# Batch 1's queries and keys on SyncE's DMA queue, channel weights gated behind them, batch 2's loads on SyncE, stores on GpSimd's queue

## The chip, the cores and the metric

One core of a Trainium2 chip runs the whole program. The metric is the device time of one execution in microseconds (us), as the median of several runs; the kernel before takes 317.31 us (median of 3 runs, 316.95 to 317.64). One more execution was taken under the hardware profiler, and all rows of a profile here come from such an execution.

## The reference

For 8 batches of 576 positions, a local attention with 8 heads of 64 channels: position i attends to j where |i - j| <= 32, or where i or j is one of 8 global positions. Its output `x` (576 x 512 per batch) goes through an MLP mixer.

```
scores = scale * q @ k.T ; attn = softmax(where(mask, scores, -1e9)) ; x = attn @ v
h   = relu(x.T @ w_tok1) @ w_tok2 ;  u = x + h.T          # mixes positions
out = u + relu(u @ w_ch1) @ w_ch2                         # mixes channels
```

q, k, v and the output are 32-bit floats, 1.18 MB per batch and tensor; the work runs in 16-bit floats.

## The kernel before, in words

**One batch at a time, overlapped.** For each batch b the loop at L956 records operations: load q, k and v into 32-bit staging tiles (`lq`, `lk`: the first 512 positions, in two DMAs of four heads, 512 KB each; `lr`: the last 64 positions of q and k, two DMAs of 128 KB; `lv`: v in five tiles), cast them to 16 bit on ScalarE (ACT) or VectorE (DVE) (`qk`, `rn`, `vsh`; L534, L531, L546), transpose q and k, compute the scores (`scores`, L673 on TensorE, PE), their exponentials (`e`, L683 on ACT), the mask (L689 on DVE), the sums over global keys (`glob_sums`: L720, which reads all five tiles of `vsh` and every head's `eg`), `rf` (L726), the attention output (`values`: L740 and L753, then `x`, L781), then `token1` (L803), `token2` (L821, `u` at L834), the transposed u (`uT`, `uTl`), `chan1` (L866, relu at L858 on ACT or L860 on DVE, which makes `b1`), `chan2` (L895, the final sum `osb` at L903) and the store (L906, L909).

**Staging tiles exist once.** `lq`, `lk`, `lr`, `lv` and `qk` have one buffer each, so that a load of batch b+1 waits until batch b was cast. `qT`, `kT`, `vsh`, `e` and `x` have two, `osb` three. The channel weights `wc1` (three DMAs of 512 output columns) and `wc2` (three) are cast from 32 to 16 bit in the DMA, which is issued from GpSimd (POOL); the token weights `w1`, `w1l`, `w2` likewise.

**Transposes.** For batches 0 to 2 PE transposes q and k (L566, L585) and u (L848). For batches 3 to 7 the DMA does: SyncE (SP) issues `raw<-qk` (L643, eight per batch), `rawr<-rn` (L639), and DVE copies them into `qT` and `kT` (L651, L654, L646, L648); `uT<-u` (L853) from batch 3 on.

**Who sets the order.** Nothing is in source order. Each `op` has a priority, candidate engines with estimated costs, and the data it reads and writes. The planner `run` (L119 to L272) simulates the engines and DMA queues with its own figures and emits the instructions in the order of that simulation; on the chip each engine then runs its list strictly in order, and waits on semaphores for the data. An `op` can also name others that it goes `behind`: that shifts it in the planner's simulation, but no semaphore comes of it, so on the chip it holds only where both stand on one engine. A `gate` (L918) is a POOL copy of one element of a loaded tile into `hold`: it makes POOL wait until that load has landed, and holds back what POOL issues next.

**Queues before.** SP issues batch 0's q, k, v, the loads of batches 3 to 7 but v, all transposes by DMA and all stores. POOL issues the gate on batch 0's v, the token weights, the gathers of global rows (L487), batch 1's q and k, then `wc1`, one part of `wc2`, batch 1's v, the rest of `wc2`, and batch 2's q, k, v. ACT issues v of batches 3 to 7. In a profile the queue of SP is q1, of POOL q0, of ACT q10. DMAs of SP and ACT use eight semaphores in turn, those of POOL eight others, and an issue waits until the last DMA on its semaphore has landed.

Of the kernel before, what the change touches and what calls it, by code (L numbers as in the profile page):

```python
# [15 lines left out]
P = 128  # L16
# [11 lines left out]
def kernel(  # L28
# [12 lines left out]
    nc = tc.nc  # L41
    B, H, S, D = q.shape
# [844 lines left out]
    def chan2(b, tau, pri):  # L887
# [17 lines left out]
        if not last:  # L905
            op([("S", 0.45)], pri + 5, lambda e: nc.sync.dma_start(out=out[b, P * tau : P * tau + P, :], in_=osb), r=[("osb", o)], dma=STORE)  # L906
        else:
            for z in range(2):
                op([("S", 0.45)], pri + 5, lambda e, z=z: nc.sync.dma_start(  # L909
                    out=out[b - 1 + z, S - LAST : S, :], in_=osb[64 * z : 64 * z + 64]), r=[("osb", o)], dma=(0.39, 2048, 0.8, 64))  # L910
# [3 lines left out]
    PEB = 3  # L914
# [7 lines left out]
    def loads(b, n0=0):  # L922
        pl = 100.0 * b - 145 if b != 1 else -174.0
        if b == 0:
            load_rest(0, -196, [("S", 0.65)])
            for hs in (slice(0, 2), slice(2, 4), slice(4, 8)):
                for ti in range(2):
                    load_qk(0, ti, hs, -195 + hs.start, [("S", 0.6)])
            load_v(0, -180, [("S", 0.6)])
            gate(-178, [("lv", NT - 4)], [lv[:, NT - 4, 0, 0:1]])  # L930
            return
        if b < PEB:
            if b == 1:
                pl = -173.9
            load_rest(b, pl, [("G", 0.73)], [n0] if b == 1 else ())
            for h in range(0, H, 4):
                for ti in range(2):
                    load_qk(b, ti, slice(h, h + 4), pl + 1 + h / 2 if b > 1 else pl + 0.1 + h / 100, [("G", 0.88)], [n0] if b == 1 else ())
            if b > 1:
                load_v(b, pl + 6, [("G", 0.87)])  # L940
        else:
            load_rest(b, pl, [("S", 0.65)])
            for h in range(0, H, 4):
                for ti in range(2):
                    load_qk(b, ti, slice(h, h + 4), pl + 1 + h / 2, [("S", 0.5)])
            load_v(b, pl + 6, [("A", 0.6)])
# [9 lines left out]
    for b in range(B):  # L956
        base = 100.0 * b
        ca = base - 85
        if b != 1:
            loads(b)  # L960
        if b == 0:
# [3 lines left out]
            n2 = len(ops) - 1  # L965
            op([("G", 0.77)], -173, f_wc1(0), w=[("wc1", 0)], dma=(2.6, 4096, 2.0, 512), behind=[n0])
            op([("G", 1.0)], -174.5, f_w2, w=["w2"], dma=(2.4, 4096, 2.0, 512), behind=[n0])
            for t in (1, 2):
                op([("G", 0.77)], -173 + t, f_wc1(t), w=[("wc1", t)], dma=(2.6, 4096, 2.0, 512), behind=[n0])
            n1 = len(ops) - 1  # L970
        if b == 1:
# [3 lines left out]
        if b < 2:  # L975
            for ti in range(2):
                op([("G", 2.7)], (-115 if ti == 0 else -174.2) if b == 0 else 70, f_gather(b, ti), r=["idx"], w=[("g32", b, ti)], dma=(0.1, 256, 1.7, 256),
                   behind=[] if b == 0 and ti == 0 else [n2])
# [80 lines left out]
```

## Time and profile before

| | |
|---|---|
| median of 3 runs | 317.31 us |
| profiled execution: its own time, its span | 317.08 us, 315.4 us |
| PE busy | 291.4 us (92%) |
| DVE, ACT, POOL busy | 187.6, 178.7, 44.5 us |
| chain of work that ended last | PE 49%, DMA 24%, DVE 11%, ACT 10% |
| DMA traffic | 51.31 MB in 96452 packets |

Times inside the execution count from the start of the span. In a timeline row stand the start, the duration, the engine, the line of the kernel, the operation, what it writes and reads, the count of merged instructions, and in brackets the idle time ahead of it with what ended it. A row of a windows table gives each engine's busy time in that stretch, then TensorE's granted clock (1.00 is full speed), the mean busy share of the 16 DMA engines (which can exceed 1 where packets overlap) and GB/s.

### The profile page before, as it was taken

Reading aid. Unit: us, or ns where it says so; the run is one execution under the profiler, and the core shown is the slowest. Engines: PE = TensorE matmul, PEld = TensorE weight load, DVE = VectorE, ACT = ScalarE, POOL = GpSimd, SP = SyncE. Lnnn points to the kernel's source line nnn. Section 1 sums busy time; section 2 is a strip of 40 time slices with the busy share of each in tenths; the row PEclk is TensorE's granted clock in tenths of the full one; section 3 lists DMA queues with packets and bytes.
Section 4 is the critical chain, followed back from the end, with each engine's and each line's share of the span. In section 5 each row is a group of like instructions: output and inputs, shape, how many; then the busy total and the mean of one; then the engine's idle time right before and its main releaser. Section 6 shows DMA issues by size and latency. Waiting matters only on the chain.

```text
span 315.4 us, 7280 instructions
## 1 busy us (share of the span) xinstructions
PE 291.4 (92%) x2944; PEld 153.3 (49%) x2944; DVE 187.6 (59%) x413; ACT 178.7 (57%) x322; POOL 44.5 (14%) x81
## 2 busy tenths in 40 slices
PE   6968989997999898999999996799999999999993
PEld 3635645453474444444475443444465445444641
DVE  7588867569777587586675657772554257230021
ACT  4872895479996484965985693541832182305500
POOL 8588735620000000000000000000000000000000
PEclk9779999999999999799999999999999999999999
DMA  6999999999599979999999989415001401051013
GB/s 179 253 135 295 207 221 246 275 254 265 122 238 214 209 207 301 162 217 223 310 164 153 304 192 203 109 22 164 33 2 31 137 35 36 11 160 49 2 67 100
DMA packets 96452, 51.31 MB, mean 163 GB/s; under 512 B 73698, under 2 KB 89954, under 8 KB 96418
## 3 DMA queue, kind: packets, MB, share of 16 engines
q1 hardware_dynamic: 66512, 33.83, 48.7%
q0 software_dynamic: 6464, 11.11, 16.5%
q10 hardware_dynamic: 23442, 5.90, 9.9%
q8 instruction: 23, 0.38, 0.5%
q14 instruction: 11, 0.09, 0.1%
HBM read 36.11 MB, written 9.44 MB: 144 GB/s over the span
## 4 chain that ended last, share of the span: by engine, by line
PE 49%; DMA 24%; DVE 11%; ACT 10%; issue 2%; SPq 2%; ACTq 1%; POOL 0%; DVEq 0%
PE bank L895 19%; PE bank L866 16%; DMA raw<-qk 9%; DMA lq<-in_q_dram 5%; DMA g_q<-in_q_dram,idx_i 4%; PE bank L821 3%; ACT e L683 3%; PE bank L803 3%; ACT b L858 3%; DMA lk<-in_k_dram 2%; PE bank L673 2%; ACT qk L534 2%; PE bank L878 2%; DVE qT L569 1%; DMA lv<-in_v_dram 1%
## 5 line engine op out<-in xcount | busy, mean ns | idle before, releaser
L866 PE MATMUL bank<-uT,wc 128*128 128x512 f16 x384 | 93.3, 384 | 3.6 <-DVE qT L589 1.3
L895 PE MATMUL bank<-wc,b 128*128 128x512 f16 x384 | 87.8, 379 | 0.1
L858 ACT ACTIVATE b<-bank 128x512 f16<-128x512 f32 x86 | 50.9, 614 | 42.8 <-PE bank L866 36.9
L683 ACT ACTIVATE e<-bank 128x648 f16<-128x648 f32 x64 | 42.8, 730 | 35.0 <-PE bank L673 33.9
L895 PEld LDWEIGHTS <-b 128*128 128x128 f16 x384 | 36.9, 98 | 43.5 <-issue 0.4
L866 PEld LDWEIGHTS <-wc 128*128 128x128 f16 x384 | 35.3, 98 | 45.1 <-issue 6.9
L903 DVE TENSOR_TENSOR osb<-u,bank 128x512 f32<-128x512 f16 x32 | 21.7, 685 | 40.5 <-PE bank L895 40.2
L689 DVE TENSOR_TENSOR e<-e,masku 128x1296 f16<-128x1296 f16 x28 | 23.2, 830 | 17.0 <-ACT e L683 16.7
L546 ACT CAST vsh<-lv 128x512 f16<-128x512 f32 (+3 forms) x44 | 27.1, 620 | 5.2 <-DMA lv<-in_v_dram 4.1
L834 DVE TENSOR_TENSOR u<-x,bank 128x512 f16<-128x512 f16 x30 | 18.7, 682 | 13.1 <-PE bank L821 12.8
L781 DVE TENSOR_TENSOR x<-bank,rr 128x512 f16<-128x512 f32 x32 | 22.1, 691 | 1.1
L740 PE MATMUL bank<-rf,lf 128*64 128x264 f16 x144 | 15.1, 278 | 5.8 <-ACT b L858 2.0
L821 PE MATMUL bank<-a,w 128*128 128x512 f16 x80 | 19.9, 379 | 0.3 <-DVE a L809 0.2
L651 DVE COPY kT<-raw 128x512 f16<-128x512 f16 x20 | 12.0, 601 | 13.5 <-DMA raw<-qk 13.4
L803 PE MATMUL bank<-x,w 128*128 128x512 f16 x64 | 19.2, 387 | 0.5 <-DMA lq<-in_q_dram 0.4
L673 PEld LDWEIGHTS <-kT 64*128 64x128 f16 x576 | 11.6, 98 | 14.7 <-issue 13.9
L534 ACT CAST qk<-lq 128x512 f16<-128x512 f32 x26 | 15.9, 623 | 4.0 <-DMA lq<-in_q_dram 4.0
L534 ACT CAST qk<-lk 128x512 f16<-128x512 f32 x27 | 16.6, 625 | 2.6 <-DMA lk<-in_k_dram 2.6
L673 PE MATMUL bank<-qT,kT 64*128 64x72 f16 x576 | 15.9, 199 | 0.5 <-ACT e L683 0.4
L753 PEld LDWEIGHTS <-e 128*64 128x64 f16 x576 | 15.3, 111 | 0.2
L753 PE MATMUL bank<-vsh,e 128*64 128x66 f16 x320 | 15.3, 194 | 0.0
L654 DVE COPY qT<-raw 128x512 f16<-128x512 f16 x20 | 11.9, 601 | 4.8 <-DMA raw<-qk 4.8
(163 smaller groups left out, 321.2 us busy)
## 6 DMA issues: line engine op xcount, KB each, us to landing
out_dram<-osb SPq DMA_DIRECT2D x32, 256.0 KB, 2.5
lq<-in_q_dram SPq DMA_DIRECT2D x11, 512.0 KB, 6.2
lk<-in_k_dram SPq DMA_DIRECT2D x11, 512.0 KB, 7.6
lv<-in_v_dram ACTq DMA_DIRECT2D x15, 256.0 KB, 5.1
wc<-in_moe_w_ch_dram POOLq DMA_DIRECT2D x6, 512.0 KB, 12.6
lq<-in_q_dram POOLq DMA_DIRECT2D x4, 512.0 KB, 12.1
lk<-in_k_dram POOLq DMA_DIRECT2D x4, 512.0 KB, 10.1
lv<-in_v_dram ACTq DMA_DIRECT2D x10, 192.0 KB, 3.9
```

The costliest lines, as they stand in the source:

```text
L534: COPY[e](out=qk[:, ti, p].rearrange("q i (r d) -> q r i d", r=2), in_=(lq, lk)[ti][:, hs])
L546: COPY[e](out=vsh[i][a:z, c, :, 0:D], in_=lv[a:z, c])
L673: nc.tensor.matmul(ps_tile[keys[z]][:, u // 3, UW * (u % 3) : UW * (u % 3) + UW], lhsT=kT[r, 64 * u : 64 * u + P], rhs=qT[r, u // 2, UW * ...
L683: op([("A", 0.595)], pri + 1, lambda e, par=par: nc.scalar.activation(out=es[i][:, 2 * p + par].rearrange("p (n u) x -> p n u x", n=3), in ...
L689: op([("V", 0.85)], pri + 2, lambda e: nc.vector.tensor_mul(out=e2, in0=e2, in1=masku.unsqueeze(1).to_broadcast([P, 2, NB, UW])), r=["mask ...
L753: nc.tensor.matmul(o[:, VW * hh : VW * hh + VW], lhsT=es[i][:, h, 2 * tau + c, x : x + 64], rhs=vod[i][:, tau, h, :] if c else vsh[i][:, t ...
L781: nc.vector.tensor_tensor(out=xo, in0=pq[:, :, :, 0:D], in1=rr.unsqueeze(3).to_broadcast([P, 2, NP, D]), op=ALU.mult,)
L803: nc.tensor.matmul(ps_tile[key][:, tt], lhsT=w, rhs=x16s[i][:, ch, :], start=(ch == 0), stop=(ch == NT - 1))
L821: nc.tensor.matmul(ps_tile[key], lhsT=w2[:, ch, P * tau - sh : P * tau - sh + P], rhs=a1[:, ch, :], start=(ch == 0), stop=(ch == 1 and not ...
L858: nc.scalar.activation(out=out, in_=in_, func=AF.Relu)
L866: nc.tensor.matmul(ps_tile[key], lhsT=wc1[:, cc, P * j : P * j + P], rhs=uT[:, cc, :], start=(cc == 0), stop=(cc == 3))
L895: nc.tensor.matmul(ps_tile[key], lhsT=w, rhs=wc2[:, j, :], start=(j == 0), stop=(j == NJ - 1))
```

## The change

Batch 1's `lr`, `lq`, `lk` are issued by SP directly behind batch 0's v. A second gate on POOL reads `lq` of batch 1 (head 4), and `wc1` and what follows on POOL go behind it. Batch 2's `lr`, `lq`, `lk` go to SP too; in the planner they stand behind the last `wc2` DMA on POOL. Batch 2's v goes to ACT's queue. The stores of batches 0 to 6 (28 DMAs of 256 KB) go from SP to POOL; those of batch 7, and those of the last 64 positions, stay on SP. Some planner figures change (0.5 to 0.55 for a load on SP, 2.3 us of `late` for the first gather).

```
-            op([("S", 0.45)], pri + 5, lambda e: nc.sync.dma_start(out=out[b, P * tau : P * tau + P, :], in_=osb), r=[("osb", o)], dma=STORE)
+            op([("G", 0.8) if b < B - 1 else ("S", 0.45)], pri + 5, lambda e: ENG[e].dma_start(out=out[b, P * tau : P * tau + P, :], in_=osb), r=[("osb", o)], dma=STORE)
...
-        if b < PEB:
-            if b == 1:
-                pl = -173.9
-            load_rest(b, pl, [("G", 0.73)], [n0] if b == 1 else ())
-            for h in range(0, H, 4):
-                for ti in range(2):
-                    load_qk(b, ti, slice(h, h + 4), pl + 1 + h / 2 if b > 1 else pl + 0.1 + h / 100, [("G", 0.88)], [n0] if b == 1 else ())
-            if b > 1:
-                load_v(b, pl + 6, [("G", 0.87)])
-        else:
-            load_rest(b, pl, [("S", 0.65)])
-            for h in range(0, H, 4):
-                for ti in range(2):
-                    load_qk(b, ti, slice(h, h + 4), pl + 1 + h / 2, [("S", 0.5)])
+        load_rest(b, pl, [("S", 0.65)], [n0] if b in (1, 2) else ())
+        for h in range(0, H, 4):
+            for ti in range(2):
+                load_qk(b, ti, slice(h, h + 4), pl + 1 + h / 2, [("S", 0.55)], [n0] if b in (1, 2) else ())
+        if b > 1:
             load_v(b, pl + 6, [("A", 0.6)])
...
-            loads(b)
+            loads(b, n3 if b == 2 else 0)
...
-            loads(1, n0)
-            op([("G", 0.77)], -40, f_wc2(0), w=[("wc2", 0)], dma=(2.6, 4096, 2.0, 512), behind=[len(ops) - 1])
+            loads(1, n0 - 1)
+            n0 = gate(-173.5, [("l", 0, 2)], [lq[:, 4, 0, 0:1]])
+            for t in range(3):
+                op([("G", 0.77)], -173 + t, f_wc1(t), w=[("wc1", t)], dma=(2.6, 4096, 2.0, 512), behind=[n0])
+            n1 = len(ops) - 1
+            op([("G", 0.77)], -40, f_wc2(0), w=[("wc2", 0)], dma=(2.6, 4096, 2.0, 512), behind=[n1])
             load_v(1, -39, [("G", 0.87)], [len(ops) - 1])
...
+            n3 = len(ops) - 1
```

What this moves in the emitted program is shown at three places.

First place, **SP's list behind batch 0's v**, changed kernel, with the semaphores that each waits for (DMAHW are the eight of SP and ACT, DMASW those of POOL; the rest are engines). The first six rows are batch 1, the next six batch 2:

```order
L514 DMA lr<-in_q_dram 64x8x64 [waits DMAHW6_49,Activation_49]
L514 DMA lr<-in_k_dram 64x8x64 [waits DMAHW7_49]
L504 DMA lq<-in_q_dram 128x4x256 [waits DMAHW0_49,Activation_49]
L504 DMA lk<-in_k_dram 128x4x256 [waits DMAHW1_49,Activation_49]
L504 DMA lq<-in_q_dram 128x4x256 [waits DMAHW2_49,DVE_49,Activation_49]
L504 DMA lk<-in_k_dram 128x4x256 [waits DMAHW3_49,DVE_49,Activation_49]
L514 DMA lr<-in_q_dram 64x8x64 [waits DMAHW6_49,DMAHW4_49,DVE_49]
L514 DMA lr<-in_k_dram 64x8x64 [waits DMAHW7_49,DMAHW5_49]
L504 DMA lq<-in_q_dram 128x4x256 [waits DMAHW0_49,Activation_49]
L504 DMA lk<-in_k_dram 128x4x256 [waits DMAHW1_49,Activation_49]
L504 DMA lq<-in_q_dram 128x4x256 [waits DMAHW2_49,Activation_49,Pool_49]
L504 DMA lk<-in_k_dram 128x4x256 [waits DMAHW3_49,DVE_49,Activation_49]
```

Before, batch 3's loads stood here, and those of batches 1 and 2 on POOL, batch 1's ahead of `wc1` and batch 2's behind the last `wc2`. Now no row of batch 2 waits for a DMASW semaphore, that is for a weight; the one wait for POOL is for the gate's copy to have read `lq`.

Second place, **ACT's list around batch 1's v**, where the relus (L858) and exponentials (L683) of the stretch stand too. Before:

```order
L683 ACTIVATE e_81<-bank 128x648 x2
L546 CAST vsh_77<-lv 32x8x64
L546 CAST vsh_77<-lv 64x8x64
L858 ACTIVATE b_100<-bank 128x512
L683 ACTIVATE e_81<-bank 128x648 x2
L546 CAST vsh_77<-lv 128x8x64 x2
L858 ACTIVATE b_100<-bank 128x512
L546 CAST vsh_77<-lv 96x8x64
L858 ACTIVATE b_100<-bank 128x512 x2
```

In the changed kernel:

```order
L683 ACTIVATE e_81<-bank 128x648 x2
L546 CAST vsh_77<-lv 128x8x64 x2
L683 ACTIVATE e_81<-bank 128x648 x2
L858 ACTIVATE b_100<-bank 128x512 x5
L523 DMA lv<-in_v_dram 96x8x64
L531 CAST rn<-lr 128x512
```

ACT now has two of the casts of v (the other three are on DVE) ahead of the last pair of exponentials, and the last five relus of batch 0 behind both.

Third place, **DVE's list at batch 5's attention** (`e_81`, `rf_86` and `x_1` are batch 5's; `raw` into `kT_75` and `qT_73` is batch 7's, into `kT_74` and `qT_72` batch 6's). Before:

```order
L654 COPY qT_73<-raw 128x4x128
L633 COPY qT_73<-gT 128x20x8
L651 COPY kT_75<-raw 128x512
L726 TENSOR_TENSOR rf_86<-bank,blk 128x528
L654 COPY qT_73<-raw 128x4x128
L651 COPY kT_75<-raw 128x512
L654 COPY qT_73<-raw 128x4x128
L780 RECIPROCAL rr_87<-bank 128x8
L781 TENSOR_TENSOR x_1_92<-bank,rr_87 128x512
```

In the changed kernel:

```order
L654 COPY qT_72<-raw 128x4x128
L633 COPY qT_73<-gT 128x20x8
L726 TENSOR_TENSOR rf_86<-bank,blk 128x528
L646 COPY qT_73<-rawr 128x4x64
L648 COPY kT_75<-rawr 128x4x64
L780 RECIPROCAL rr_87<-bank 128x8
L781 TENSOR_TENSOR x_1_92<-bank,rr_87 128x512
```

Batch 7's eight copies from `raw` all stood ahead of batch 5's first `x` before; now they stand behind its last one and ahead of its `u` (L834); batch 6's last three stand ahead of `rf`.

More of the change, by code (lines that the diff above doesn't have):

```diff
@@ L976 @@
             for ti in range(2):
-                op([("G", 2.7)], (-115 if ti == 0 else -174.2) if b == 0 else 70, f_gather(b, ti), r=["idx"], w=[("g32", b, ti)], dma=(0.1, 256, 1.7, 256),
-                   behind=[] if b == 0 and ti == 0 else [n2])
+                op([("G", 2.7)], (-115 if ti == 0 else -174.2) if b == 0 else 70, f_gather(b, ti), r=["idx"], w=[("g32", b, ti)], dma=(0.1, 256, 1.7, 256), late=0.0 if b or ti else 2.3,
+                   behind=[n3] if b else [n2] if ti else [])
         casts(b)
```

6 lines of the change are left out of this document (1 added, 5 removed).

## The prediction

> **What bounds the kernel now.** I read the page first: who is busy, and the chain that ended last.
>
> ```profile
> PE 291.4 (92%) x2944; PEld 153.3 (49%) x2944; DVE 187.6 (59%) x413; ACT 178.7 (57%) x322; POOL 44.5 (14%) x81
> ...
> PE 49%; DMA 24%; DVE 11%; ACT 10%; issue 2%; SPq 2%; ACTq 1%; POOL 0%; DVEq 0%
> ```
>
> PE is the bound where it has work; the change moves no arithmetic and can only win or lose PE's idle time, 315.4 - 291.4 = 24 us of the span. Then the windows, to see where that idle time lies (the second number is PE's busy time in the 20 us).
>
> ```profile
> 100.00:120.00 20.00, 18.83 (x168) 9.18 (x169) 15.25 (x30) 13.14 (x25) 0.00 (x0) 1.00 1.09 227
> 120.00:140.00 20.00, 17.99 (x174) 8.86 (x172) 13.62 (x33) 14.33 (x26) 0.00 (x0) 0.91 1.31 225
> 140.00:160.00 20.00, 20.00 (x244) 9.96 (x243) 13.74 (x27) 14.52 (x29) 0.00 (x0) 1.00 1.16 253
> 180.00:200.00 20.00, 15.20 (x234) 8.22 (x232) 11.90 (x27) 12.96 (x24) 0.00 (x0) 1.00 0.96 208
> ```
>
> PE is full from 140 to 160 and loses 4.8 us from 180 to 200, 1.2 and 2.0 us in the two windows ahead. So an early delay is not simply kept: it is kept where PE is full, and swallowed where PE would have waited for transfers anyway. The last question is how full the DMA engines are early on, since the change reorders their work (last two columns: busy share, GB/s).
>
> ```profile
> 17.00:25.00 8.00, 5.94 (x118) 3.58 (x119) 6.21 (x17) 4.43 (x9) 7.39 (x12) 0.79 0.87 132
> 25.00:31.00 6.00, 5.14 (x75) 3.11 (x72) 5.73 (x18) 1.83 (x4) 5.42 (x8) 1.00 0.99 333
> ```
>
> From 17 to 25 us they carry the token weights and the gathers, busy 0.87 of the time but at 132 GB/s; from 25 to 31, with batch 1's q and k, they carry 333 GB/s.
>
> **Part 1: batch 1's q and k start earlier.** Before, the last of batch 0's v and the last of batch 1's k land as follows.
>
> ```profile
> L523 SPq DMA_DIRECT2D lv<-in_v_dram x2: 1216/1319/1422, 12.0 to 13.2; - x2
> ...
> DMA to landing us min/median/max: 5.3/5.5/5.7
> ```
>
> ```profile
> L504 POOL DMA_DIRECT2D lk<-in_k_dram x2: 791/792/793, 23.5 to 24.9; - x2
> ...
> DMA to landing us min/median/max: 7.1/7.1/7.1
> ```
>
> That is 13.2 + 5.3 = 18.5 and 24.9 + 7.1 = 32.0. Now batch 1's 2.36 MB (four DMAs of 512 KB, two of 128 KB) run behind v, beside the token weights. The room beside these is (1 - 0.87) x 8 = 1.0 us by busy share and (333 - 132) / 333 x 8 = 4.8 us by bytes, so the last k lands between 27.2 and 31.0; I take 29.5, near the middle. The trace doesn't show which end holds. PE can use little of it. In the changed kernel the transposes of batch 1 stand inside `token1` of batch 0, and batch 0's `a1` behind the last casts of batch 1, so batch 0's chain waits for that landing, and the first `chan1` (36.38 us before) still needs the first third of `wc1`, which the gate lets go only when q's second half is there, one 512 KB transfer (0.52 / 333 = 1.6 us) ahead of the last k, at about 28 us.
>
> ```profile
> 36.38 0.81 PE L866 MATMUL bank<-uT,wc 128*128 128x512 f16 x3
> 25.69 2.29 POOL L474 DMA_DIRECT2D wc<-in_moe_w_ch_dram  x3
> ```
>
> Before, `wc1` was issued at 25.69, but stood in one queue behind a k that landed at 32.0; now its flow begins about 1 us earlier. I cost this part at nothing, between -2.5 (all of the earlier landing is won) and +1.5 (the token weights, which now share the engines, come late for `token1`).
>
> **Part 2: batch 2's q, k are not behind the weights on the chip.** The order rows show no wait for a weight in them. As soon as batch 1 is cast, near 26 to 30 us, they are issued, and run beside `wc1`, `wc2` and batch 1's v. That two queues share the engines is seen where SP's first load of batch 3 met POOL's loads of batch 2:
>
> ```profile
> L514 SPq DMA_DIRECT2D lr<-in_q_dram x1: 601/601/601, 56.1 to 56.1; - x1
> ...
> DMA to landing us min/median/max: 13.3/13.5/13.6
> ```
>
> A 128 KB load took 13 us: SP's queue did get on while POOL's was full, but slowly. Batch 2's load is 2.36 MB, at 333 GB/s 7.1 us of the engines. About 1.1 us of it runs before `wc1` flows. So batch 1's v, last in POOL's queue, which before landed at 36.4 + 12.3 = 48.7,
>
> ```profile
> L523 POOL DMA_DIRECT2D lv<-in_v_dram x1: 793/793/793, 36.4 to 36.4; - x1
> ...
> DMA to landing us min/median/max: 12.3/12.3/12.3
> ```
>
> lands at 48.7 - 1.0 + 7.1 - 1.1 = 53.7. The bounds: 47.7, if POOL's queue is served first, and 54.8, if all of batch 2 goes ahead. I take the even sharing. Before, v was used at once:
>
> ```profile
> 46.96 1.31 ACT L683 ACTIVATE e<-bank 128x648 f16<-128x648 f32 x2
> 48.29 1.14 ACT L546 CAST vsh<-lv 128x512 f16<-128x512 f32 x2
> 49.83 0.60 ACT L546 CAST vsh<-lv 96x512 f16<-96x512 f32 x1
> 50.33 1.07 ACT L858 ACTIVATE b<-bank 128x512 f16<-128x512 f32 x2
> ```
>
> ```profile
> 50.66 0.47 PE L720 MATMUL bank<-vsh,eg 128*32 128x132 f16 x20
> 51.06 1.04 PE L895 MATMUL bank<-wc,b 128*128 128x512 f16 x4
> 52.36 0.42 PE L740 MATMUL bank<-rf,lf 128*64 128x264 f16 x4 [0.26 <-DVE rf L726]
> ```
>
> The last cast began at 49.83 and L720 ran at 50.66. Now ACT has the casts of v's third and fourth tile ahead of the last pair of exponentials, and these ahead of five relus. The fourth tile lands about 1 us before the last, at 52.7; cast 0.6, two exponentials 1.3, five relus at about 0.55 make 57.4; then L895 (which needs every relu) 1.0, so L740 starts at 58.4 instead of 52.36: **+6.0 us**, from -1 to +7.2 by the bounds.
>
> **Part 3: what of this later waits swallow.** Behind 52 us PE is nearly full up to these rows:
>
> ```profile
> 72.98 0.81 PE L866 MATMUL bank<-uT,wc 128*128 128x512 f16 x3 [1.33 <-DVE qT L589]
> 110.34 1.02 PE L866 MATMUL bank<-uT,wc 128*128 128x512 f16 x4 [1.17 <-DVE osb L903]
> 69.41 0.23 DVE L617 CAST g_q<-g_q 128x128 f16<-128x128 f32 x1 [1.80 <-DMA g_q<-in_q_dram,idx_i]
> ```
>
> At 72.98 PE waits for a DVE that had stood at 69.41 for a gather, with batch 2's v behind. The cast of that gather is now ACT's, and batch 2's q, k are there long before: **-1.3**. At 110.34 it waits for an `osb` that stood behind copies of `raw`; PE arrives late anyway: **-1.2**. The 2.0 us from 120 to 140 (ACT held up by batch 5's load) I leave as they are, since SP's list puts that load behind batch 4's transposes again.
>
> **Part 4: stores off SP, and the order of 180 to 200.** Here PE waits for DVE and ACT, which wait for transfers of work that is far ahead:
>
> ```profile
> 192.06 0.46 PE L720 MATMUL bank<-vsh,eg 128*32 128x132 f16 x17 [1.09 <-DVE eg L692]
> 195.71 0.42 PE L740 MATMUL bank<-rf,lf 128*64 128x264 f16 x4 [1.36 <-DVE rf L726]
> 199.72 0.30 PE L740 MATMUL bank<-rf,lf 128*64 128x264 f16 x2 [1.89 <-DVE x L781]
> 194.45 0.60 DVE L651 COPY kT<-raw 128x512 f16<-128x512 f16 x1 [1.23 <-DMA raw<-qk]
> 197.71 0.60 DVE L651 COPY kT<-raw 128x512 f16<-128x512 f16 x1 [1.53 <-DMA raw<-qk]
> 194.32 0.60 ACT L858 ACTIVATE b<-bank 128x512 f16<-128x512 f32 x1 [5.44 <-DMA lv<-in_v_dram]
> 183.82 0.69 DVE L903 TENSOR_TENSOR osb<-u,bank 128x512 f32<-128x512 f16 x1 [0.23 <-DMA out_dram<-osb]
> ```
>
> DVE stands at 194.45 and 197.71 for batch 7's transposes, ahead of batch 5's `rf` and `x`; ACT stands 5.44 us behind a load of v that waits for its semaphore. In the changed kernel batch 7's copies stand behind batch 5's last `x`, and 28 stores, of which some stood between transposes on SP and took turns on the eight semaphores, are on POOL. I count all 4.8 us of the window as won. A gain above that isn't there; the other end is 0, if batch 6's copies or ACT's issues of v hold them up as long. On POOL the stores are hidden by its idleness (busy 0.00 in the windows above from 100 us on) and by three `osb` buffers; without that cover each would cost DVE its landing time.
>
> **The sum**, against the profiled execution's 317.08 us (span 315.4 and 1.7 around it): 0 + 6.0 - 1.3 - 1.2 - 4.8 = -1.3, so 315.8; that execution stands 0.23 below the median of 317.31, so **316.0 us** as a median.
>
> **Rivals.** (a) *The early loss is kept*: batch 6's last copies, still ahead of `rf`, and ACT's issues of v put a wait of the same size in the place of the one removed, 4.8 us. Then 317.31 + 6.0 - 1.3 - 1.2 = 320.8. For it speaks that batch 6's last three transposes now stand behind the four of batch 4's `u` in SP's list; against it that DVE no longer waits for batch 7 there. It ends slower from the point where less than 3.5 of the 4.8 us are won. (b) *Batch 2 doesn't hold up the weights*: POOL's queue is served first, as the 13 us of SP's small load would also allow. Then the change does what it says, part 2 costs -1 to 0, and the time is 317.31 - 1.3 - 1.2 - 4.8 = 310.0. (c) *Stores on POOL come late*: at 183.82 DVE's fourth `osb` of a batch already waited for a store. If POOL's issue is held until a DVE instruction of 0.83 us (L689) is over, up to 0.83 x 7 batches = 5.8 us come on top: 321.8. Against it: from 25 to 31 us DVE was busy for 5.73 of 6 us, and POOL issued three `wc` DMAs in 2.29 us, 0.76 each, as it had at quieter times. The Trainium skill, SBUF — State Buffer, section "Summary: rules for kernel authors", says the same as this rival: to hide a DMA under a DVE operation it wants it on ACT's or SP's queue, since GpSimd cannot write descriptors while DVE holds the shared port in its fast modes. By that rule the sum would be (c)'s; the rows above speak against it here.
>
> **How the numbers follow.** About 0.2% (0.6 us) is what a measurement of this kernel can tell from no change. Forecast: 0.44, its own range 313.5 to 317.6, of which 0.31 faster, 0.09 within 0.2%, 0.04 slower. (a) 0.36, slower. (b) 0.14, faster. (c) 0.06, slower. Together: faster 0.45, same 0.09, slower 0.46. The signs are nearly even: the early loss is worked out from rows that hang together, the later gain from an order that changes. The range 311 to 322 takes in (a) with its spread and most of (b).
>
> **What would show it.** In the profile after: batch 2's `lq` landing before batch 1's `lv` (part 2), PE waiting several us ahead of L720 or L740 near 50 to 58 us, with ACT's exponentials or relus behind a cast of `vsh`; no wait for `qT` L589 near 78; from 180 to 200 PE busy 19 us or more, and DVE's `rf` of batch 5 without a wait for `raw` ahead of it. If L740 of batch 1 starts by 53 us, part 2 is wrong and (b) holds; if the wait near 190 is still 4 us, (a) does.

## The result, and the profile after

The changed kernel takes 321.39 us (median of 4 runs, 319.36 to 323.76), the kernel before in the same runs 317.13 us (4 runs, 314.88 to 317.64): a ratio of 1.0146, with a 95% interval of 1.0097 to 1.0194. It is slower by 4.3 us at the medians, against a forecast of 316.0; rival (a) had said 320.8. The interval reaches half a per cent to either side, so noise is larger here than the 0.2% that the prediction reckoned with. The profiled execution took 320.91 us with a span of 319.2.

The page of the changed kernel, as of before: busy times, and the chain that ended last.

```profile
PE 291.1 (91%) x2934; PEld 152.5 (48%) x2934; DVE 183.5 (57%) x408; ACT 183.0 (57%) x327; POOL 46.3 (15%) x93
...
PE 53%; DMA 27%; DVE 9%; ACT 5%; SPq 3%; issue 2%; POOL 0%; ACTq 0%; DVEq 0%
```

PE's work is the same, its idle time is 319.2 - 291.1 = 28.1 us instead of 24.0. The windows say where (the second number is PE's busy time). First two of the kernel before, then those of the changed kernel:

```profile
20.00:40.00 20.00, 17.88 (x255) 11.03 (x253) 15.90 (x39) 12.49 (x26) 16.19 (x24) 0.96 1.04 228
40.00:60.00 20.00, 18.94 (x236) 9.92 (x236) 14.23 (x30) 13.17 (x25) 11.05 (x13) 1.00 1.12 255
```

```profile
20.00:40.00 20.00, 14.16 (x192) 9.31 (x193) 12.40 (x31) 11.77 (x24) 8.39 (x11) 0.91 1.15 271
40.00:60.00 20.00, 17.11 (x220) 8.01 (x220) 9.96 (x21) 13.38 (x26) 7.85 (x14) 0.91 1.11 213
60.00:80.00 20.00, 19.78 (x170) 10.64 (x168) 13.60 (x28) 11.20 (x21) 2.10 (x4) 1.00 0.74 212
100.00:120.00 20.00, 17.53 (x129) 8.16 (x128) 10.99 (x20) 12.01 (x23) 2.17 (x4) 1.00 0.98 215
120.00:140.00 20.00, 18.77 (x215) 9.68 (x215) 17.08 (x41) 14.48 (x25) 0.00 (x0) 1.00 1.14 231
140.00:160.00 20.00, 17.34 (x135) 7.67 (x136) 14.44 (x26) 10.60 (x19) 2.47 (x4) 1.00 1.06 253
180.00:200.00 20.00, 18.88 (x234) 9.34 (x234) 14.34 (x29) 14.85 (x28) 1.63 (x3) 1.00 1.11 234
200.00:220.00 20.00, 18.53 (x126) 8.58 (x122) 16.10 (x30) 9.68 (x17) 1.12 (x2) 1.00 0.84 154
```

From 20 to 60 PE lost 3.7 + 1.8 = 5.5 us. From 180 to 200 it gained 18.88 - 15.20 = 3.7 us, nearly what part 4 said. But from 140 to 160, where it had been full, it lost 2.7 us, from 100 to 120 1.3 and from 200 to 220 1.5. Over the whole stretch from 100 to 220, before and after:

```profile
100.00:220.00 120.00, 111.95 (x1088) 55.83 (x1089) 79.53 (x160) 73.90 (x134) 0.00 (x0) 0.99 0.99 198
```

```profile
100.00:220.00 120.00, 110.71 (x1065) 55.02 (x1064) 83.90 (x168) 78.56 (x139) 7.92 (x14) 1.00 1.06 211
```

111.95 became 110.71: the wait from 180 to 200 went, and a little more came back beside it. Each row is from one execution, but three other kernels with the new order, described below, agree: 110.52 in after_b2_held, 110.90 in after_b2_pool, 111.15 in after_stores_sp. In the early part, batch 1's v and L740 came as the forecast said. Batch 1's v in the changed kernel, and ACT's row of its casts:

```profile
L523 POOL DMA_DIRECT2D lv<-in_v_dram x5: 794/909/921, 32.4 to 39.4; - x5
...
DMA to landing us min/median/max: 14.8/17.8/18.6
```

```profile
49.00 1.34 ACT L683 ACTIVATE e<-bank 128x648 f16<-128x648 f32 x2
52.60 0.62 ACT L546 CAST vsh<-lv 128x512 f16<-128x512 f32 x1 [2.26 <-DMA lv<-in_v_dram]
53.60 0.62 ACT L546 CAST vsh<-lv 128x512 f16<-128x512 f32 x1 [0.38 <-DMA lv<-in_v_dram]
54.12 1.30 ACT L683 ACTIVATE e<-bank 128x648 f16<-128x648 f32 x2
```

The last v lands at 39.4 + 14.8 = 54.2 (53.7 was forecast); ACT stands 2.26 us for the third tile and 0.38 us for the fourth, with the exponentials behind them. PE's rows, from the timeline, at eight places:

```profile
21.64 0.40 PE L585 MATMUL bank<-ident,rn 128*128 128x128 f16 x4 [2.23 <-DVE rn L531]
...
38.89 3.67 PE L866 MATMUL bank<-uT,wc 128*128 128x512 f16 x11 [2.29 <-DMA wc<-in_moe_w_ch_dram]
...
54.88 1.02 PE L866 MATMUL bank<-uT,wc 128*128 128x512 f16 x4 [2.24 <-ACT e L683]
...
56.57 0.46 PE L720 MATMUL bank<-vsh,eg 128*32 128x132 f16 x17 [0.50 <-DVE eg L692]
...
58.15 0.30 PE L740 MATMUL bank<-rf,lf 128*64 128x264 f16 x2 [0.15 <-DVE rf L726]
...
147.24 5.34 PE L895 MATMUL bank<-wc,b 128*128 128x512 f16 x24 [2.34 <-DVE osb L903]
...
183.61 4.04 PE L895 MATMUL bank<-wc,b 128*128 128x512 f16 x18 [1.12 <-DVE osb L903]
...
219.04 4.04 PE L895 MATMUL bank<-wc,b 128*128 128x512 f16 x18 [1.04 <-DVE osb L903]
```

The first row was not forecast: PE stands 2.23 us for the cast of batch 1's `rn`, ahead of batch 0's attention output. In the kernel before, the same L585 stood at 28.83 and didn't wait. L740 of batch 1 starts at 58.15 (58.4 forecast, 52.36 before). What it waits for last is not the forecast's chain of five relus and L895: the last exponentials are followed on DVE by their mask, `eg` (which ends L720's wait) and `rf` (which ends L740's).

The last three rows are new: PE waits for `osb`. DVE's rows ahead of the wait at 183.61:

```profile
179.37 0.61 DVE L654 COPY qT<-raw 128x512 f16<-128x512 f16 x1 [2.20 <-DMA raw<-qk]
179.89 2.48 DVE L834 TENSOR_TENSOR u<-x,bank 128x512 f16<-128x512 f16 x4
182.28 0.68 DVE L837 TENSOR_TENSOR ul<-x,bank 64x512 f16<-64x512 f16 x1
182.88 0.68 DVE L903 TENSOR_TENSOR osb<-u,bank 128x512 f32<-128x512 f16 x1
```

DVE waits 2.20 us for a transpose (`raw`) of a batch ahead, and batch 4's five `u` and then `osb` stand behind it. But this alone is no new thing. In the kernel before, batch 4's `u` stood behind such a wait too, and PE had no wait for `osb` there:

```profile
172.16 0.61 DVE L654 COPY qT<-raw 128x512 f16<-128x512 f16 x1 [1.64 <-DMA raw<-qk]
172.80 2.48 DVE L834 TENSOR_TENSOR u<-x,bank 128x512 f16<-128x512 f16 x4
```

The copies that the change took away from batch 5's `rf` and `x` stand at 204 to 212 us in the changed kernel, ahead of batch 5's `u`:

```profile
208.44 0.61 DVE L651 COPY kT<-raw 128x512 f16<-128x512 f16 x1 [2.06 <-DMA raw<-qk]
...
211.29 0.60 DVE L651 COPY kT<-raw 128x512 f16<-128x512 f16 x1 [0.59 <-DMA raw<-qk]
211.92 2.48 DVE L834 TENSOR_TENSOR u<-x,bank 128x512 f16<-128x512 f16 x4
```

With one more wait of 0.52 at 210.09 they stand 3.2 us for transposes. Of the three waits for `osb` only the last, 1.04 us at 219.04, comes behind them.

### The profile page after: what moved, and what is told of

Read it like the earlier page. It is cut to its first block, busy times and chain, and to the rows that moved or that the text cites. A ratio compares the mean times of both kernels' runs of the same rounds, so it can differ in the third digit from the quotient of the medians.

```text
span 319.2 us, 7239 instructions
## 1 busy us (share of the span) xinstructions
PE 291.1 (91%) x2934; PEld 152.5 (48%) x2934; DVE 183.5 (57%) x408; ACT 183.0 (57%) x327; POOL 46.3 (15%) x93
## 3 DMA queue, kind: packets, MB, share of 16 engines
q10 hardware_dynamic: 28130, 7.08, 12.5%
## 4 chain that ended last, share of the span: by engine, by line
PE 53%; DMA 27%; DVE 9%; ACT 5%; SPq 3%; issue 2%; POOL 0%; ACTq 0%; DVEq 0%
PE bank L895 19%; PE bank L866 16%; DMA rawr<-rn 8%; DMA lv<-in_v_dram 8%; PE bank L803 4%; DMA lq<-in_q_dram 3%; PE bank L878 3%; DMA lr<-in_k_dram 3%; PE bank L821 3%; PE bank L740 2%; ACT vsh L546 2%; PE bank L753 2%; SPq L523 2%; PE bank L673 2%; DMA wc<-in_moe_w_ch_dram 2%
## 5 line engine op out<-in xcount | busy, mean ns | idle before, releaser
L866 PE MATMUL bank<-uT,wc 128*128 128x512 f16 x384 | 93.3, 384 | 4.9 <-DMA wc<-in_moe_w_ch_dram 2.3
L895 PE MATMUL bank<-wc,b 128*128 128x512 f16 x384 | 88.0, 379 | 4.5 <-DVE osb L903 4.5
L858 ACT ACTIVATE b<-bank 128x512 f16<-128x512 f32 x88 | 51.6, 608 | 40.3 <-PE bank L866 40.2
L895 PEld LDWEIGHTS <-b 128*128 128x128 f16 x384 | 37.0, 98 | 48.6 <-issue 5.7
L683 ACT ACTIVATE e<-bank 128x648 f16<-128x648 f32 x64 | 42.3, 720 | 28.2 <-PE bank L673 28.1
L866 PEld LDWEIGHTS <-wc 128*128 128x128 f16 x384 | 35.1, 98 | 46.4 <-issue 5.6
L906 POOL DMA_DIRECT2D out_dram<-osb x28 | 15.6, 556 | 221.5 <-DVE osb L903 221.5
L834 DVE TENSOR_TENSOR u<-x,bank 128x512 f16<-128x512 f16 x30 | 18.7, 681 | 17.9 <-PE bank L821 17.9
L546 ACT CAST vsh<-lv 128x512 f16<-128x512 f32 (+3 forms) x41 | 24.6, 623 | 6.6 <-DMA lv<-in_v_dram 5.3
L534 ACT CAST qk<-lq 128x512 f16<-128x512 f32 x30 | 17.7, 619 | 8.9 <-DMA lq<-in_q_dram 7.9
L740 PE MATMUL bank<-rf,lf 128*64 128x264 f16 x144 | 15.8, 296 | 1.3 <-DVE rf L726 0.9
```

The source lines that it names most:

```text
L534: COPY[e](out=qk[:, ti, p].rearrange("q i (r d) -> q r i d", r=2), in_=(lq, lk)[ti][:, hs])
L546: COPY[e](out=vsh[i][a:z, c, :, 0:D], in_=lv[a:z, c])
L683: op([("A", 0.595)], pri + 1, lambda e, par=par: nc.scalar.activation(out=es[i][:, 2 * p + par].rearrange("p (n u) x -> p n u x", n=3), in ...
L740: nc.tensor.matmul(o[:, 0 : NP * VW], lhsT=lf[:, P * tau + 64 * c : P * tau + 64 * c + 64], rhs=rf[:, 2 * hf : 2 * hf + 2], start=start, s ...
L858: nc.scalar.activation(out=out, in_=in_, func=AF.Relu)
L866: nc.tensor.matmul(ps_tile[key], lhsT=wc1[:, cc, P * j : P * j + P], rhs=uT[:, cc, :], start=(cc == 0), stop=(cc == 3))
```

## The experiments

Eighteen runs, each timed in five rounds beside the kernel before on the same chip. The kernel before had medians of 317.5 to 318.6 us in them, so the ratios (with 95% intervals) are compared; 1% is 3.2 us. "Order kept" means that the planner simulates the same program and so emits every list in the same order, and only the emission (L243, `o["fn"](e)`) puts an instruction on another queue or place. `b1s`, `b2` are the sets of batch 1's and batch 2's six loads of q and k.

| run | median, us | ratio to before | L740 of batch 1, us |
|---|---|---|---|
| changed kernel | 321.39 | 1.0146 (1.0097 to 1.0194) | 58.2 |
| after_b2_held | 318.73 | 1.0017 (0.9981 to 1.0053) | 53.5 |
| after_b2_pool | 316.86 | 0.9963 (0.9930 to 0.9997) | 53.2 |
| after_stores_sp | 323.61 | 1.0185 (1.0130 to 1.0239) | 58.0 |
| after_u_first | 323.36 | 1.0185 (1.0131 to 1.0239) | 59.0 |
| after_b2_pool_u_first | 318.32 | 1.0014 (0.9969 to 1.0060) | 51.9 |
| after_casts3_early | 324.54 | 1.0255 (1.0179 to 1.0332) | 59.4 |
| after_casts3_on_pool | 323.69 | 1.0180 (1.0140 to 1.0220) | 60.1 |
| after_casts_on_pool | 325.17 | 1.0230 (1.0192 to 1.0268) | 58.2 |
| change_without_part2 | 334.08 | 1.0569 (1.0490 to 1.0647) | 57.3 |
| before_b1_sp | 318.12 | 1.0045 (1.0002 to 1.0088) | 53.3 |
| before_b2_early | 320.85 | 1.0097 (1.0060 to 1.0135) | 59.4 |
| before_stores_pool | 314.87 | 0.9902 (0.9866 to 0.9939) | 52.7 |
| before_all_queues | 320.71 | 1.0039 (0.9980 to 1.0099) | 56.1 |
| before_rf_first | 315.39 | 0.9951 (0.9913 to 0.9989) | 53.4 |
| before_stores_pool_rf_first | 313.58 | 0.9845 (0.9780 to 0.9911) | 52.9 |
| before_stores_replan | 316.02 | 0.9954 (0.9910 to 0.9998) | 51.7 |
| before_fewer_stores | 313.93 | 0.9857 (0.9792 to 0.9923) | 52.5 |
| before_extra_loads | 323.82 | 1.0163 (1.0091 to 1.0235) | 52.4 |

### Part 2: batch 2's loads against the weights

My theory after the result was that batch 2's traffic makes the early loss; the rival was that the new order and the later gate make it. after_b2_held holds the loads on SyncE by a data dependence:

```
-            o["fn"](e)
+            i == min(b2, default=-1) and nc.gpsimd.tensor_copy(out=lr[:, 0, 0:1], in_=wc2[:, NJ - 1, 0:1]); o["fn"](e)
```

> The changed kernel with its order of instructions kept on every engine; added is one GpSimd copy of an element of the last part of wc2 into lr, so that SyncE's loads of batch 2 wait until the channel weights have landed. Traffic theory (batch 2's 2.36 MB took the engines from wc1, wc2 and batch 1's v, and that is the loss): the first L866 starts at 35 to 36.5 us instead of 38.9, batch 1's lv lands by 49 instead of 54.2, L740 of batch 1 starts at 52.5 to 54 instead of 58.15, and the kernel takes about 317 us instead of 321.4 (a loss of 4 to 5 us gone). Order theory (the new order of the first 60 us, with batch 1's transposes inside batch 0's chain and wc1 issued 3.5 us later by the gate, makes the loss by itself): L740 of batch 1 still starts at 57 us or later, and the time stays above 320.

after_b2_pool issues them from GpSimd instead, `o["fn"]("G" if i in b2 else e)`:

> The changed kernel with its order kept, batch 2's six loads of q and k issued from GpSimd behind the last wc2 DMA, as before the change. Traffic theory: as in the run with the loads held, about 317 us, L740 of batch 1 at 52.5 to 54 us; if only the queue's choice of packets mattered and not the time of the loads, the two runs would differ by over 1 us. Order theory: L740 at 57 us or later, above 320 us.

In both the loss is all but gone: 1.0017 and 0.9963 instead of 1.0146. Batch 1's v in the run with the loads held:

```profile
L523 POOL DMA_DIRECT2D lv<-in_v_dram x5: 794/949/958, 32.8 to 37.1; - x5
...
DMA to landing us min/median/max: 12.4/12.6/13.3
```

The last one needs 12.5 us and lands at 37.1 + 12.5 = 49.6 instead of 54.2, and L740 starts 4.7 us earlier (53.47). So does the wait for `wc1` at 38.89 go; the first L866 of that run waits for a copy on ACT:

```profile
37.38 2.75 PE L866 MATMUL bank<-uT,wc 128*128 128x512 f16 x12 [0.67 <-ACT uT L850]
```

The gate, which issues `wc1` 3.5 us later than before, stands in this run too; so it was not what made PE wait for `wc1`. The converse, before_b2_early, puts the same six loads on SyncE in the kernel before, `o["fn"]("S" if i in b2 else e)`:

> The kernel before with its order kept, only batch 2's six loads of q and k issued by SyncE instead of GpSimd (they wait for batch 1's casts and for nothing of the weights). Traffic theory: the loads start at 26 to 32 us, batch 1's lv lands 4 to 6 us later than 48.6, L740 of batch 1 starts at 56 to 58 us instead of 52.36, and the time is 319 to 322 us. Order theory: lv lands where it did within 1.5 us, 316.5 to 318 us.

1.0097, and the five loads of v need 19.1 to 22.0 us, against 12.3 to 15.4 before:

```profile
L523 POOL DMA_DIRECT2D lv<-in_v_dram x5: 793/889/956, 28.1 to 36.1; - x5
...
DMA to landing us min/median/max: 19.1/21.7/22.0
```

```profile
51.77 6.31 PE L866 MATMUL bank<-uT,wc 128*128 128x512 f16 x16 [6.29 <-ACT b L858]
...
59.38 0.42 PE L740 MATMUL bank<-rf,lf 128*64 128x264 f16 x4
```

Part 2 is shown both ways: taken out of the changed kernel, and put into the old one. L740 is 7.0 us late here, the end only 1.0097, 3.1 us: the old order swallows over half. In the changed kernel 58.15 - 53.47 = 4.7 us of delay come to 4.1 us at the end (1.0146 - 1.0017), and against after_b2_pool 58.15 - 53.20 = 4.9 us come to 5.8 us: there nothing is seen to be swallowed, though the intervals leave room for about 2 us either way.

### The stores, and batch 1's loads, alone

after_stores_sp puts the 28 stores back, `o["fn"]("S" if o["dma"] is STORE else e)`:

> The changed kernel with its order kept, only the 28 stores issued by SyncE again instead of GpSimd. Stores theory (the new waits of PE for osb at 147, 184 and 219 us, 5 us in sum, come from stores on GpSimd's queue that free an osb buffer late): these waits fall below 1 us in sum and the time is 316.5 to 318 us. Order theory (DVE makes osb late because copies of raw stand ahead of u and osb in its list, and waits for a transpose): the waits stay within 1 us, and the time is 320 to 324 us, with stores between transposes on SyncE costing 0 to 2 us.

before_stores_pool does the reverse in the kernel before, for all 32 stores of 256 KB:

> The kernel before with its order kept, only its 32 stores of 256 KB issued by GpSimd instead of SyncE. Theory that stores on GpSimd are hidden and unload SyncE: transposes land earlier or as before, 0 to 2 us faster than the kernel before. Rival (c) of the prediction (GpSimd's issue is held up by DVE, so that osb comes free late): DVE waits for stores at L903, 2 to 6 us slower.

before_b1_sp makes part 1 alone:

```
+            i in wcf and nc.gpsimd.tensor_copy(out=hold[:, 0:1], in_=lq[:, 4, 0, 0:1]); o["fn"]("S" if i in b1s else e)
```

> The kernel before with its order kept, only batch 1's six loads of q and k issued by SyncE behind batch 0's v, and the gate on lq of batch 1 ahead of wc1. Theory that part 1 is free: wc1 lands first between 33.5 and 36 us, batch 1's v within 1.5 us of 48.6, L740 of batch 1 starts at 51 to 53.5, and the time is within 1 us of the kernel before. Rival (the loads share the engines with the token weights, and the gate lets wc1 go 3.5 us later): L740 at 54 us or later, and 1.5 to 3 us slower.

The stores are no loss on GpSimd: 0.9902 in the old order is a gain of 3.1 us, and taking them back in the changed kernel gains nothing (1.0185 against 1.0146, with intervals that overlap). That refutes rival (c) and my later theory that the new waits for `osb` come from late stores: with the stores back on SyncE three such waits are still there (3.7 us in sum, 4.5 in the changed kernel). Part 1 costs 0.1 to 2.8 us by its interval, 1.4 in the middle.

### What part 4 counted, alone

before_rf_first moves batch 7's copies of `raw` behind batch 5's last `x` in DVE's list, as the changed kernel has them, and nothing else (`zone` is set from batch 5's last mask to that `x`):

```
+        if zone[0] and i in rawc:
+            held.append((i, e))
+            return
```

> The kernel before with the order of all engines but DVE's kept: batch 7's copies of raw that stood between batch 5's last mask and its last x now stand behind that x, as in the changed kernel. Part 4 of the prediction (PE's 4.8 us of idle time from 180 to 200 are won when rf and x no longer stand behind these copies): 312.5 to 314.5 us. Theory of the moved wait (the copies wait for the same transposes at their new place, ahead of u, so that PE waits for u and osb instead): within 1.2 us of the kernel before.

```profile
180.00:200.00 20.00, 19.65 (x256) 10.03 (x255) 13.52 (x31) 14.03 (x26) 0.00 (x0) 1.00 1.03 208
```

PE's window rises from 15.20 to 19.65, 4.45 us; the time falls by 1.6 us (0.9951, by its interval 0.3 to 2.8 us). That lies between the two expectations: about a third of the wait is won. Over 100 to 220 us this execution has PE busy for 112.56 us against 111.95, so even with every other list kept the window's gain is not the stretch's. Then both edits of part 4 in the old order, stores on GpSimd and these copies:

> The kernel before with two edits that were each faster alone: stores on GpSimd in the old order (-2.6 to -3.1 us) and batch 7's copies of raw behind batch 5's last x (-1.6 to -2.1 us). If the two win different waits: 312 to 313.5 us. If both win the same one (SyncE's transposes that DVE waits for from 180 to 200): 314.5 to 316 us.

0.9845, 4.9 us faster (2.8 to 7.0): the two gains add up (0.9902 x 0.9951 = 0.985). This is the lowest ratio of all these kernels, clearly below the kernel before and the changed one; its interval overlaps with that of the stores alone. Its stretch from 100 to 220:

```profile
100.00:220.00 120.00, 115.20 (x1144) 57.32 (x1142) 83.00 (x167) 77.77 (x142) 8.46 (x15) 1.00 1.01 199
```

### Queues or order

before_all_queues has all three moves of queues in the order of before, with both sets and the stores in one line:

```
+            i in wcf and nc.gpsimd.tensor_copy(out=hold[:, 0:1], in_=lq[:, 4, 0, 0:1]); o["fn"]("G" if o["dma"] is STORE else "S" if i in b1s or i in b2 else e)
```

> The kernel before with the order of its list kept, and all three moves of queues in it: batch 1's q and k on SyncE with the gate on lq ahead of wc1, batch 2's q and k on SyncE, the 32 stores of 256 KB on GpSimd (batch 2's v stays on GpSimd). It has the changed kernel's queues in the old order. Sum of the parts measured alone (+0.7 to +1.4, +2.9, -2.6 to -3.1): 318 to 319 us; then the new order costs the 2.5 to 3.5 us that are left to 321.4. If the queues alone make the loss: 320.5 to 322 us, and the new order is worth nothing either way.

1.0039, just what the parts alone make (1.0045 x 1.0097 x 0.9902 = 1.0043). The rest up to 1.0146, 1.1% or 3.4 us, is the new order of the lists (and batch 2's v on ACT's queue, which I did not run apart). By the ends of the two intervals it can be anything from 0 to 6.8 us; without part 2 it is smaller, since after_b2_pool at 0.9963 stands near 1.0045 x 0.9902 = 0.9947. How much an order can weigh was tried with two kernels that the planner was let order anew. before_stores_replan has the store line of the change in the kernel before; change_without_part2 is the change with batch 2's q, k, v on GpSimd, in the planner's figures too:

> The kernel before with one line of the change: the 28 stores of batches 0 to 6 on GpSimd, in the planner too, which makes a new order. If the gain of 1 per cent that the stores gave in the old order carries over: 313.5 to 316 us. If a new order costs more than that: 317 us or more.

> The changed kernel, but batch 2's q, k and v on GpSimd behind the last wc2 DMA, in the planner too. If part 2 is what makes the change slower, and the rest is worth what it gave alone (stores -3, batch 1 on SyncE +0.5 to +1.4): 314 to 316.5 us. If the new order of the rest costs by itself: 317.5 us or more.

The first shows no clear cost of its new order: 0.9954 against the 0.9902 of the stores in the old order, with intervals that overlap, and single times from 311.5 to 318.4 us. The second is clear: 1.0569, with the same queues as after_b2_pool but for batch 2's v, and a time 17 us longer. In the list of PE's waits of that kernel (us in total, times, longest) no single row explains it:

```profile
PE bank L673 <- ACT e L683: 4.5, 5, 1.5
PE bank L585 <- DVE rn L531: 4.0, 1, 4.0
PE bank L740 <- DVE rf L726: 3.5, 3, 1.6
PE bank L566 <- ACT uT L850: 2.8, 1, 2.8
```

### Where the new order loses: what was tried, and what stays open

First, the copies of `raw` ahead of `u`. after_u_first and after_b2_pool_u_first hold them back, in DVE's list alone, until the first `osb` behind a batch's `u`:

```
+        if zone[0] and i in rawc:
+            held.append((i, e))
+            return
```

> The changed kernel, all engines' orders kept but DVE's: copies of raw (L651, L654) that stood between a batch's last x and the first osb behind its u now stand behind that osb. Theory of the moved wait (what the new order gave at 180 to 200 us it took back because DVE, held by copies of a transpose that lands late, makes u and osb late, so that PE waits at L895 for 2.5, 1.3 and 1.2 us near 147, 184 and 219): these three waits fall to under 1.5 us in sum, and the time falls from 321.4 to 317.5 to 319.5 us. Rival (the copies are needed soon anyway, by the scores of the next batch but one, or PE waits for transposes in any order): the waits come back at L673, L740 or L866 and the time stays above 320.5 us.

> The same order of DVE, with batch 2's six loads on GpSimd behind the last wc2 DMA as in the run of 316.86 us. Theory of the moved wait: the waits of L895 for osb (2.5, 1.2 and 1.2 us there) fall to under 1.5 us in sum, and the time to 313 to 315 us, below the kernel before. Rival: 316 to 318 us.

My theory fell: 1.0185 and 1.0014, no faster than without the edit. In after_b2_pool_u_first the three waits are now these two:

```profile
147.14 2.64 PE L866 MATMUL bank<-uT,wc 128*128 128x512 f16 x8 [1.97 <-DMA uT<-u]
...
214.84 4.05 PE L895 MATMUL bank<-wc,b 128*128 128x512 f16 x18 [2.94 <-DVE osb L903]
```

The wait is still there; only what ends it has another name. Nor do these waits tell a slow kernel from a fast one: after_b2_pool (0.9963) has three for `osb`, 4.4 us in sum, nearly the 4.5 of the changed kernel (1.0146). What makes them is not shown.

Is it the DMA engines, then, that pace this stretch? before_fewer_stores leaves out the 16 stores of batches 2 to 5 (`i in mid or o["fn"](e)`), before_extra_loads adds 16 loads that nothing reads:

> The kernel before without the 16 stores of batches 2 to 5 (256 KB each; their rows 0 to 511 are left out of the output). If the DMA engines set PE's lost time between 100 and 220 us (8.1 us there before): 4.2 MB and 16 issues on SyncE less give 3 to 6 us. If latencies and the lists of DVE and ACT set it: like the run with stores on GpSimd, 2 to 3 us from SyncE's free list and no more.

> The kernel before with 16 loads of 256 KB more, issued by GpSimd into a tile that nothing reads, each when an osb of batches 2 to 5 has been made. If the DMA engines set PE's lost time between 100 and 220 us: 4.2 MB more, at 333 GB/s 12.6 us of the engines, of which the half or more would show: 4 to 10 us slower. If they do not: within 1.5 us of the kernel before.

4.2 MB less give 4.5 us (0.9857), 4.2 MB more cost 5.2 us (1.0163), though the extra loads are issued by a GpSimd that is nearly idle there (each with a one-element copy that waits for the `osb`). The stretch with the extra loads:

```profile
100.00:220.00 120.00, 107.78 (x1042) 54.96 (x1043) 80.33 (x162) 73.25 (x132) 8.89 (x19) 0.97 1.05 212
```

If all of it is traffic, it has a price of 1.1 to 1.2 us per MB there, an estimate from the middles of wide intervals (0.6 to 1.8). Part of the gain of the first run is SyncE's free list: moving all 32 stores to GpSimd already gave 3.1 us. In the changed kernel the DMA engines stand half idle from 80 to 100 us (share 0.58; 0.87 before): ACT casts batch 3's `rn` at 88.28, and SyncE issues the first transpose `rawr` behind it at 88.94 instead of 73.65. Three runs start that work earlier, with batch 3's nine casts (`c3`) further ahead in ACT's list, `rn` before batch 2's copies of `kT` (`t2`) and q and k before its exponentials, or those casts on GpSimd, or all casts of batches 3 to 7 on GpSimd:

```
+    move(c3[0], t2)
...
+        ops[y[0]]["fn"]("G" if y[0] in c3 else y[1])
```

> The changed kernel with the order of all engines but ACT's kept: on ACT the cast of batch 3's rn and its eight casts of q and k move from among and behind the relus of batch 2's chan1 (88 to 97 us) to between batch 2's copies of kT and its exponentials (74 to 87 us). Theory of the paced middle (from 100 to 200 us the DMA engines are busy more than all the time, and the changed kernel started that work 15 us later, rawr of batch 3 at 88.9 instead of 73.7, so that whichever engine stands last waits for it): rawr of batch 3 is issued near 74, batch 4's loads before 95 instead of 102, PE loses 3 to 5 us less between 100 and 220, and the time is 316.5 to 318.5 us. Rival (ACT's late casts are harmless, only what stands ahead of what on DVE counts): above 320.5 us.

> The changed kernel with batch 3's nine casts (rn, q, k) on GpSimd at the earlier place, so that ACT's list loses them instead of having them ahead of its exponentials (which cost 3 us in the run with them early on ACT). Theory of the paced middle: rawr of batch 3 is issued by 79 instead of 88.9, PE waits for no exponential at 83 to 94, and the time is 317 to 320 us against the 321.4 of the changed kernel. Rival (where batch 3's casts stand doesn't matter, batch 4's set the pace again): 320.5 to 323 us. GpSimd's time for a cast, and what it costs DVE beside it, is in no row so far and could hide a gain.

> The same with the casts of batches 3 to 7 on GpSimd (batch 3's at the early place, the others where ACT had them). Theory of the paced middle: with ACT free of 45 casts at 0.62 us each and the casts bound by the landing of their loads alone, PE's lost time from 100 to 220 falls from 9.3 to under 6 us and the time to 315 to 319 us. Rival: above 320.5 us; if a GpSimd cast takes over 2 us, the transposes come late and the kernel is slower than the changed one.

All three are slower or the same: 1.0255, 1.0180, 1.0230. From 100 to 220 PE was busier in all of them (114.20, 115.39 and 113.11 us instead of 110.71), most in the run with batch 3's casts on GpSimd:

```profile
60.00:100.00 40.00, 36.85 (x354) 19.15 (x354) 26.15 (x45) 21.78 (x39) 7.34 (x13) 0.88 0.68 162
100.00:220.00 120.00, 115.39 (x1206) 59.79 (x1205) 85.96 (x178) 81.81 (x145) 6.79 (x12) 1.00 1.01 204
```

but PE lost 3.2 us from 60 to 100 (0.2 in the changed kernel) to what the casts held up. A loss ahead of the stretch can make the waits in it shorter, so its higher figure is no proof of a gain, and the edits carried a cost of their own. The same execution also had PE busy for only 42.94 us in the first 60, where the edit moves nothing yet, against 45.99 in the changed kernel: windows of single executions can differ by 3 us without any edit.

Which list of the new order makes its 3.4 us stays open. One place that no run tried is on PE's list near 22 us: every profile of a kernel with the changed kernel's order, and change_without_part2, has the wait of L585 for batch 1's `rn` (2.2 to 4.3 us), and the kernel before and those in its order have none. What it costs at the end is not measured.

## Why the prediction was wrong, point by point

- **Part 1** (0, from -2.5 to +1.5): +1.4 us alone, inside the bounds but at their upper end (0.1 to 2.8 by its interval). The last k, issued at 19.55, landed 11.3 us later at 30.8, not at 29.5: the bound by busy share held. That `wc1` would come as early as before is nearly right once batch 2 is away: its first third landed at 38.9 in the changed kernel, at 36.5 in after_b2_held and 35.0 in after_b2_pool, against 34.5 before. That batch 1's transposes stand inside batch 0's chain was read in the lists but given no price of its own; PE's wait of 2.23 us for `rn` at 21.64 comes of it.
- **Part 2** (+6.0 at L740): right in the mechanism up to the exponentials, since v landed at 54.2 against 53.7 and ACT's exponentials stood behind its cast. Behind them the chain was another (mask, `eg`, L720, `rf` instead of five relus and L895), and it began later, with the cast of the fourth tile at 53.60 instead of 52.7; that the two errors nearly cancel, 58.15 against 58.4, is luck. Rival (b) is refuted by the landing of v.
- **Part 3** (-1.3 and -1.2): right in size in the old order, where 7.0 us at L740 come to 3.1 at the end, but only one of its two waits went there: in before_b2_early the wait of L866 for `qT` near 73 is gone, and that of L866 for `osb`, at 116.08 there, is still 1.2 us. In the changed kernel the wait at 72.98 went as said (the window from 60 to 80 rose from 18.37 to 19.78), but that from 100 to 120 grew instead of shrinking (18.83 to 17.53).
- **Part 4** (-4.8) is the step that failed: "I count all 4.8 us of the window as won." In the changed kernel most of the window was won (15.20 to 18.88, 3.7 us), but a window's gain was taken for the time's. With the 1.2 us of part 3's second wait, the forecast had 6.0 us less idle time on PE from 100 to 220 us; the profile has 1.2 us more, with 4.5 us in waits of L895 for `osb`, of which the kernel before has none. The prediction gave no price to what the same reordering does to `u`, `osb` and the rest of the stretch. Its two edits, the stores and batch 7's copies, are worth 4.9 us together in the order of before, though the copies alone, which won the window, are worth only 1.6. Why the new order takes the gain back stays open: the copies of `raw` ahead of `u`, the stores and the late casts of batch 3 were each moved without a gain.
- **The sum**: parts 1 to 3, measured alone in the old order, make 1.4 + 3.1 = +4.5 us (3.5 was forecast), and the changed kernel stands at +4.6 by its ratio: priced so, part 4 came to nothing in sum. Part 2 priced in the new order is 4.1 to 5.8 us (against after_b2_held and after_b2_pool), and then 0.9 to 2.6 us of part 4 are left and part 3 swallowed less. How the miss is shared between parts 3 and 4 thus depends on the order in which one measures.
- **Rivals**: (a) had the time, 320.8 for 321.4, and the right idea, a wait of the same size in the place of the one removed; its place was wrong (no copy of `raw` ahead of `rf` waited from 180 to 200; the new waits were for `osb`). (c) is refuted by the stores alone on GpSimd, 3.1 us faster. The Trainium skill, SBUF — State Buffer, section "Summary: rules for kernel authors", wants a DMA that is to be hidden under a DVE operation on ACT's or SP's queue; here GpSimd's queue was the better one for the stores. The likely reason is that GpSimd was idle from 100 us on in the kernel before (busy 0.00 us in the windows) while SyncE's list was full of transposes; no run tested it apart.

## What to carry to other kernels

A gain that is read from one window is not yet a gain in time: 4.45 us in a window were worth 1.6 us in before_rf_first, and 3.7 us in the changed kernel nothing over the stretch. Price the place where a moved instruction lands like the one that it leaves, and count over the whole stretch. Where a planner decides the order, test a change of queues in the old order first (queues 1.0039, with the new order 1.0146, though by the ends of the intervals the two can be equal; and one replanned kernel 1.0569), and keep the order if it is the better one. Loads that are issued early because nothing on the chip holds them back are not free: what is needed next shares the DMA engines with them. A planner's "behind" doesn't hold them; a data dependence does (after_b2_held), and so does a place behind the weights in the same queue (after_b2_pool).

## What the runs showed of the hardware that was not expected

A row of casts on GpSimd held up a DVE operation with two inputs until the row was over. In the run with batch 3's casts on GpSimd, the first and the last of eight back-to-back casts, DVE's mask beside them, and PE behind that:

```profile
83.29 0.62 POOL L534 CAST qk<-lq 128x512 f16<-128x512 f32 x1
...
87.19 0.60 POOL L534 CAST qk<-lk 128x512 f16<-128x512 f32 x1
```

```profile
83.66 4.82 DVE L689 TENSOR_TENSOR e<-e,masku 128x1296 f16<-128x1296 f16 x1 [0.60 <-ACT e L683]
```

```profile
91.30 1.01 PE L866 MATMUL bank<-uT,wc 128*128 128x512 f16 x2 [2.93 <-DVE b L860]
```

The mask takes 0.83 us in the kernel before (mean of 28); here 4.82, and it ends 0.7 us after the last cast. PE then waited 2.93 us, which is most of what this run lost from 60 to 100. The Trainium skill, SBUF — State Buffer, section "Terms", says that DVE and GpSimd share one pair of ports, by an exclusive lock that is held for a whole instruction. The trace agrees that one waits for the other, and goes further: this mask did not get its turn between the eight casts. It is the one such event in this run; with the casts of batches 3 to 7 on GpSimd the 28 masks took 28.4 us in sum instead of 23.2. On the other hand a cast in this row was as quick on GpSimd (0.60 to 0.62 us) as on ACT (0.62).
